# Row maxima of two heads in one step, one head in each row half of the array

## The chip, the cores and the metric

The kernel runs on one core of a Trainium2 chip. The metric is the device time of one execution in microseconds (us). Three runs of the kernel before took 3167.71, 3168.49 and 3175.28 us; the median is 3168.49 us.

## The reference, cut to what matters

Four residual layers work on 2048 rows of 512 numbers. Layers one and three (A) are attention with 32 query heads and one shared key/value head. Layers two and four (B) have 32 heads of 16 numbers each and cut the rows into 4 segments of 512: within a segment the attention is causal, and a running memory of the earlier segments is mixed in. The change touches only B's causal part:

```
for s in range(N):                                    # N = 4 segments of L = 512 rows
    qs, ks, vs = q[:, :, s], k[:, :, s], v[:, :, s]
    logits = jnp.einsum("bhqd,bhkd->bhqk", qs, ks) * scale + mask
    p = _softmax(logits, axis=-1)
    a_dot = jnp.einsum("bhqk,bhkd->bhqd", p, vs)
    ...
    o = g * a_mem + (1.0 - g) * a_dot
```

The logits of B are large, so the kernel needs the maximum of each row of logits (each head, each of the 512 rows of a segment, over the keys up to that row) before it takes exponentials.

## The kernel before, in words

**The work.** Rows come in 4 blocks of 512 (a block is a segment of B). One block of layer B, with the output projection of A ahead of it and its own behind it, is a "side" (`side`, L1182). Seven of the eight sides are woven with the scores and products of layer A for the next block (`weave`, L427); the eighth runs alone at the end. In a side B's 32 heads form 8 units of 4 heads, n = 0 to 7. The four heads j of a unit are (u, i), j = 2u + i: i says in which row half of the array the head's numbers lie (partitions 0 to 47 or 64 to 111 of `qkb`), u which of two column buffers it uses.

**The row maxima** (`b_rowmax`, L964; `b_rowmax_masked`, L942, in the last side). Query rows go in four tiles qt of 128, and tile qt meets nk = 128(qt+1) keys. For a head and a tile, `by_pairs` (L110) with one half issues four matmuls of 32 columns each, which write one PSUM bank: 48 rows of one row half of the array, four column groups. VectorE then reduces the bank. Unmasked, this is an instruction pair per head and tile (L988: add the causal mask, take the maximum into `mo`, then read the accumulator into `m`), 16 pairs for a unit. A job is what shares one bank: `(3, j)` with 512 keys; `(2, j)` and `(0, j)` with 384 and 128; two heads of tile 1 with 256 each. That makes 10 jobs for a unit, each with a bank of its own. In the last side the mask is added by four more matmuls (`maskw`), and VectorE needs a plain reduction (L959), 12 for a unit.

**The guard.** `guard_rows` (L681) transposes the maxima on TensorE (L687), VectorE splits them into two fp16 numbers (L690 to L693), and DMAs over `mf` put them into rows 48 and 49 of the half of `qkb` that each head uses. Only then can `b_attend` (L999) issue the scores of that unit (50 rows, `by_pairs` with both halves, eight matmuls into two banks, mask by `maskv`), the exponentials on ScalarE (L1027, `pa`), the products with the values (`b_pv`, L1068, reading `vb`) and the transposes on VectorE (L1038, L1047).

**The banks.** A ring hands out PSUM: "sc" holds two-bank slots for scores, "r" single banks for everything else (projections, row maxima, guards, products, transposes). `layout` (L359) gives "r" two banks (4 and 5) while a side is woven with A, eight at the start of the last side and four in the rest of it.

**What sets the order.** The program is written once, by a planner that keeps a clock per engine. Each generator yields the time at which its next step could start (`Need`, L371; a bank is ready HOP = 250 after the planned end of its reduction); `par` (L386), `step` and `weave` choose the next step by these times, by the array's tiling form and by how far A and the side have come. The row maxima of unit n+2 are planned beside unit n (`b_block`, L1138). Planned costs: `cols(nk)` per head and tile on TensorE, 65 + 1.05 per key on VectorE. Engines run their instructions in the order in which this leaves them, apart from a reach of 400 that `together` (L96) gives to the later matmuls of a group.

Of the kernel before, what the change touches and what calls it, by code (L numbers as in the profile page):

```python
# [31 lines left out]
BF16 = mybir.dt.bfloat16  # L32
# [3 lines left out]
ALU = mybir.AluOpType  # L36
AX = mybir.AxisListType

P = 128
# [50 lines left out]
def net_kernel(ctx, tc, x_in, a_wq, a_wk, a_wv, a_wo, b_wq, b_wk, b_wv, b_wo, b_beta, cst, out):  # L90
    nc = tc.nc
    V, A, G = nc.vector, nc.scalar, nc.gpsimd
# [3 lines left out]
    def together(first, *a, **k):  # L96

        if first:
            nc.tensor.matmul(*a, **k)  # L99
        else:  # L100
            with tc.high_priority(offset=400):
                tc.keep_in_program_order(nc.tensor.matmul(*a, **k))  # L102

    def by_columns(first, out_, lhsT, rhs, **k):

        for c in (2, 3, 0, 1):
            r_ = slice(32 * c, 32 * c + 32)
            together(first and c == 2, out_[r_], lhsT=lhsT[:, r_], rhs=rhs, **k)

    def by_pairs(out_, lhsT, rhs, rows=49, halves=(0, 1), mask=None):  # L110

        o = lambda r_, i: out_[r_, i] if len(halves) == 2 else out_[r_]
        for c in (2, 3, 0, 1):
            r_ = slice(32 * c, 32 * c + 32)
            for i in halves:
                w_ = slice(64 * i, 64 * i + rows)
                together(c == 2 and i == halves[0], o(r_, i), lhsT=lhsT[w_, r_], rhs=rhs[w_], start=True, stop=mask is None)
        if mask is None:
            return
        m_, a = mask  # L120
        for c in (2, 3, 0, 1):
            r_ = slice(32 * c, 32 * c + 32)
            for i in halves:
                w_ = slice(64 * i, 64 * i + 64)
                together(False, o(r_, i)[:, a:a + P], lhsT=idb[w_, 64 * i:64 * i + 32], rhs=m_[w_, c, :],
                         start=False, stop=True)

    def by_triangle(first, out_, lhsT, rhs):
# [19 lines left out]
    def nm(s):  # L148
        uid[0] += 1
        return f"{s}_{uid[0]}"  # L150

    def st(shape, dt, tag):
        return one.tile(shape, dt, tag=tag, name=nm(tag))

    def tmp(n, shape, dt, tag):
        return pools[n].tile(shape, dt, tag=tag, name=nm(tag))
# [5 lines left out]
    HOP = 250.0  # L162
# [10 lines left out]
    def pe(cost, form="full"):  # L173
        clk["pe"] += cost + (DRAIN if form != tiling[0] else 0.0)
        tiling[0] = form
        return clk["pe"]

    def on(engine, after, cost):
        clk[engine] = max(clk[engine], after + HOP) + cost
        return clk[engine] - NEAR[engine]  # L180
# [24 lines left out]
    maskq = st([P, 512], BF16, "maskq")  # L205
# [3 lines left out]
    idb = st([P, P], BF16, "idb")  # L209
# [8 lines left out]
    maskw = st([P, 4, P], BF16, "maskw")  # L218
# [116 lines left out]
    def cols(n, passes=1):  # L335
        return max(n * passes / 2.4, 107.0) + 3

    class Ring:
# [2 lines left out]
        def __init__(self, slots):  # L341
            self.slots, self.free = slots, [0.0] * len(slots)

        def ready(self):
            return min(self.free) + HOP

        def take(self):
            i = min(range(len(self.free)), key=lambda j: self.free[j])
# [8 lines left out]
    rings = {}  # L357
# [323 lines left out]
    def guard_rows(m, q, ring, exact):  # L681

        k, ps = ring.take()
        if len(ps.shape) == 3:
            ps = ps[:, 0, :]
        ps = ps[0:16, 0:P]
        T.transpose(ps, m.rearrange("p a b -> p (a b)"), ident)  # L687
        if not exact:
            mr = tmp(2, [16, 2, P], F16, "mrr")
            V.tensor_scalar_mul(mr[:, 0, :], ps, 1.0 / GUARD_K)  # L690
            V.scalar_tensor_tensor(mr[:, 1, :], ps, 1.0 / GUARD_K, mr[:, 0, :], op0=ALU.mult, op1=ALU.subtract)
            V.tensor_reduce(mmx[:, 1:2], ps, axis=AX.X, op=ALU.max, apply_absolute_value=True)
            V.tensor_tensor(mmx[:, 0:1], mmx[:, 0:1], mmx[:, 1:2], op=ALU.max)  # L693
            md = dram.tile([2, 16, P], F16, tag="mf" + str(uid[0] % 4), name=nm("mf"))
            nc.sync.dma_start(md.rearrange("o t c -> t o c"), mr)
            for i in range(2):
                nc.sync.dma_start(q[64 * i + 48:64 * i + 50].rearrange("o u (t c) -> o u t c", t=4),
                                  md.rearrange("o (u i t) c -> i o u t c", u=2, i=2)[i])
            t = on("dve", pe(110, "full"), 700)
            ring.free[k] = t  # L700
            return t + 2 * LOAD
        mr = tmp(2, [16, 2, P], BF16, "mrr")
        V.tensor_copy(mr[:, 0, :], ps)
        V.tensor_tensor(mr[:, 1, :], ps, mr[:, 0, :], op=ALU.subtract)
        md = dram.tile([2, 16, P], BF16, tag="md" + str(uid[0] % 4), name=nm("md"))
        nc.sync.dma_start(md.rearrange("o t c -> t o c"), mr)
        nc.sync.dma_start(q[96:98].rearrange("o j c -> o (j c)"), md.rearrange("o t c -> o (t c)"))
        t = on("dve", pe(110, "cols"), 350)
        ring.free[k] = t
        return t + 2 * LOAD  # L710
# [231 lines left out]
    def b_rowmax_masked(n, need):  # L942

        q, k = qb[n % 3], kb[n % 3]
        m = tmp(2, [P, 2, 2, 4], F32, "m")
        for qt in (3, 2, 1, 0):
            nk = (qt + 1) * P
            per = min(512 // nk, 2)
            for i in range(2):
                for u0 in range(0, 2, per):  # L950
                    yield Need(lambda: max(need, rings["r"].ready()), "rows")
                    ring = rings["r"]
                    s, ps = ring.take()
                    for u in range(per):
                        o_ = u * nk
                        by_pairs(ps[:, o_:o_ + nk], q[:, u0 + u, qt * P:(qt + 1) * P], k[:, u0 + u, 0:nk], 48, (i,),
                                 (maskw, nk - P))
                        e = pe(cols(nk) + 57, "rows")
                    V.reduce_max(m[:, u0:u0 + per, i, qt], ps[:, 0:per * nk].rearrange("p (h k) -> p h k", k=nk), axis=AX.X)  # L959
                    ring.free[s] = on("dve", e, 65 + 1.05 * per * nk)  # L960
        yield rings["r"].ready
        gr[n] = guard_rows(m.rearrange("p u i t -> p (u i) t"), q, rings["r"], False)

    def b_rowmax(n, need, exact=False):  # L964

        q, k = (qx, kx) if exact else (qb[n % 3], kb[n % 3])
        m = tmp(2, [P, 4, 4], F32, "m")
        jobs = [[(3, j)] for j in range(4)] + [[(2, j), (0, j)] for j in range(4)] + [[(1, 0), (1, 2)], [(1, 1), (1, 3)]]
        for job in jobs:
            yield Need(lambda: max(need, rings["r"].ready()), "cols" if exact else "rows")  # L970
            ring = rings["r"]
            s, ps = ring.take()
            o_ = 0
            for qt, j in job:
                nk = (qt + 1) * P
                if exact:
                    by_columns(o_ == 0, ps[:, o_:o_ + nk], q[0:96, j, qt * P:(qt + 1) * P], k[0:96, j, 0:nk],
                               start=True, stop=True)
                else:
                    u, i = divmod(j, 2)  # L980
                    by_pairs(ps[:, o_:o_ + nk], q[:, u, qt * P:(qt + 1) * P], k[:, u, 0:nk], 48, (i,))
                o_ += nk
                e = pe(cols(nk), "cols" if exact else "rows")
            o_ = 0
            for qt, j in job:
                nk = (qt + 1) * P
                mo = tmp(1, [P, 512], BF16, "mo")
                V.tensor_tensor_reduce(out=mo[:, 0:nk], in0=ps[:, o_:o_ + nk], in1=maskq[:, 512 - nk:512],  # L988
                                       op0=ALU.add, op1=ALU.max, scale=1.0, scalar=-3.0e38,
                                       accum_out=m[:, j, qt:qt + 1])  # L990
                o_ += nk
                e = on("dve", e, 65 + 1.05 * nk)
            ring.free[s] = e
        yield rings["r"].ready
        gr[n] = guard_rows(m, q, rings["r"], exact)

# [99 lines left out]
    def b_block(b, last, exact, norms):  # L1096
# [8 lines left out]
        def rowmax(*units):  # L1105
            for n in units:
                if n < 8:
                    need = b_load(hold[n // 2], n)
                    yield from b_rowmax(n, need, True) if exact else (b_rowmax_masked if last else b_rowmax)(n, need)
# [131 lines left out]
    ps = one_[0][0:1, 0:1]  # L1241
# [35 lines left out]
```

## Time and profile before

| | |
|---|---|
| median of three runs | 3168.49 us |
| the profiled execution | 3173.05 us, of which its span is 3170.8 us |
| granted TensorE clock, mean | 0.974 |
| busy: PE, ScalarE (ACT), VectorE (DVE) | 2804.4, 2328.1, 1553.0 us |
| row maxima on DVE: L988 (56 units of the seven woven sides) | 896 reductions, 438.7 us |
| row maxima on DVE: L959 (8 units of the last side) | 96 reductions |

PE is TensorE's matmuls, PEld its weight loads. The time that a wait took stands behind the group or instruction that waited, with what it waited for. Matmul durations in the trace are from the start to the modelled end of one matmul, and neighbouring ones overlap; how fast the array takes work is read from the distance between starts. The prediction shows the rows on which it rests.

### The profile page before, as it was taken

Reading aid. Unit: us, or ns where it says so; the run is one execution under the profiler, and the core shown is the slowest. Engines: PE = TensorE matmul, PEld = TensorE weight load, DVE = VectorE, ACT = ScalarE, POOL = GpSimd, SP = SyncE. Lnnn points to the kernel's source line nnn. Section 1 sums busy time; section 2 is a strip of 40 time slices with the busy share of each in tenths; the row PEclk is TensorE's granted clock in tenths of the full one; section 3 lists DMA queues with packets and bytes.
Section 4 is the critical chain, followed back from the end, with each engine's and each line's share of the span. In section 5 each row is a group of like instructions: output and inputs, shape, how many; then the busy total and the mean of one; then the engine's idle time right before and its main releaser. Section 6 shows DMA issues by size and latency. Waiting matters only on the chain.

```text
span 3170.8 us, 115988 instructions
## 1 busy us (share of the span) xinstructions
PE 2804.4 (88%) x51714; PEld 1329.7 (42%) x51714; DVE 1553.0 (49%) x4463; ACT 2328.1 (73%) x2583; POOL 269.5 (8%) x437
## 2 busy tenths in 40 slices
PE   7978898899888998889998898988998899888987
PEld 3533344344443454334443344443443434433543
DVE  7611345534565445554365545564345533654465
ACT  4699787886788867887788878767687876878423
POOL 3100120001000010001100010000000000000011
PEclk9999999999999999999999999999999999999978
DMA  5310231123311233102321142320331114110331
GB/s 157 113 61 20 75 111 45 38 64 100 91 48 29 67 108 93 48 16 93 122 85 50 35 143 86 111 67 23 112 94 36 38 49 127 46 48 22 121 99 34
DMA packets 147837, 231.84 MB, mean 73 GB/s; under 512 B 29728, under 2 KB 97152, under 8 KB 147328
## 3 DMA queue, kind: packets, MB, share of 16 engines
q1 hardware_dynamic: 118912, 121.56, 13.2%
q0 software_dynamic: 28416, 102.77, 10.1%
q8 instruction: 407, 6.67, 0.9%
q14 instruction: 102, 0.84, 0.1%
HBM read 162.12 MB, written 62.13 MB: 71 GB/s over the span
## 4 chain that ended last, share of the span: by engine, by line
PE 34%; ACT 27%; issue 22%; DVE 9%; DMA 5%; POOL 2%; SPq 1%; DVEq 0%; ACTq 0%; POOLq 0%
ACT pa L751 23%; PE bank L99 15%; PE bank L454 11%; PE bank L102 7%; DVE mo L988 4%; ACT pa L1027 3%; DMA sb<-parts 2%; DVE m L959 1%; DVE parts L552 1%; DMA xt<-in_A_x_dram 1%; DMA qkb<-sb 1%; POOL parts L550 0%; POOL w L275 0%; DMA w<-wd 0%; PE bank L687 0%
## 5 line engine op out<-in xcount | busy, mean ns | idle before, releaser
L751 ACT ACTIVATE pa<-bank 128x1024 f32<-128x1024 f32 x2048 | 1946.6, 1111 | 468.5 <-PE bank L102 464.4
L102 PE MATMUL bank<-pa,va 64*17 64x512 f32 x14336 | 1107.9, 602 | 0.2 <-DVE t L790 0.2
L99 PE MATMUL bank<-pa,va 64*17 64x512 f32 x2048 | 1065.0, 601 | 8.9 <-DVE ts L789 4.6
L99 PE MATMUL bank<-qa,kst 49*32 49x512 f16 x2048 | 745.0, 383 | 173.2 <-ACT pa L751 144.2
L102 PE MATMUL bank<-qa,kst 49*32 49x512 f16 x14336 | 825.1, 388 | 1.7 <-DVE qmx L599 1.7
L988 DVE CUSTOM_DVE_ANT_0 mo<-bank,maskq 128x256 bf16<-128x256 f32 (+3 forms) x896 | 438.7, 490 | 239.6 <-PE bank L102 177.8
L99 PE MATMUL bank<-qkb 48*32 48x512 f16 (+7 forms) x1536 | 347.7, 310 | 114.0 <-DVE m L988 44.9
L102 PEld LDWEIGHTS <-kst 49*32 49x32 f16 x14336 | 228.4, 90 | 496.3 <-issue 485.6
L1027 ACT ACTIVATE pa<-bank 128x1024 f32<-128x1024 f32 (+2 forms) x384 | 323.0, 887 | 139.5 <-PE bank L102 137.1
L102 PE MATMUL bank<-qkb 48*32 48x384 f16 (+7 forms) x6656 | 370.4, 313 | 0.0
L99 PEld LDWEIGHTS <-kst 49*32 49x32 f16 x2048 | 173.6, 92 | 370.9 <-issue 345.0
L454 PE MATMUL bank<-xh,w 128*128 128x512 f32 x832 | 284.4, 406 | 8.5 <-DVE w L318 5.0
L102 PEld LDWEIGHTS bank<-pa,va 64*17 64x17 f32 x14336 | 258.9, 95 | 25.5 <-DVE t L790 9.1
L454 PE MATMUL bank<-w,xh 128*128 128x512 f32 x752 | 247.8, 409 | 4.7 <-issue 3.1
L102 PEld LDWEIGHTS <-qkb 48*32 48x32 f16 (+1 forms) x6656 | 153.7, 94 | 202.7 <-issue 194.3
L99 PEld LDWEIGHTS bank<-pa,va 64*17 64x17 f32 x2048 | 186.6, 94 | 103.2 <-issue 18.2
L99 PEld LDWEIGHTS <-qkb 48*32 48x32 f16 (+1 forms) x1536 | 130.2, 95 | 172.5 <-issue 139.0
L789 DVE STREAM_TRANSPOSE ts<-bank 128x512 f32<-128x512 f32 x88 | 62.9, 714 | 276.4 <-PE bank L102 276.0
L275 POOL DMA_DIRECT2D w<-wd x154 | 85.4, 554 | 1253.2 <-PE bank L454 1166.7
L454 PEld LDWEIGHTS bank<-xh,w 128*128 128x128 f32 x832 | 156.8, 189 | 76.2 <-issue 29.7
L102 PE MATMUL bank<-pa,vb 128*17 128x384 f32 (+3 forms) x1920 | 173.9, 444 | 8.6 <-ACT pa L1027 7.7
L1038 DVE STREAM_TRANSPOSE t<-bank 128x512 f32<-128x512 f32 x64 | 45.9, 717 | 249.8 <-PE bank L102 249.8
(164 smaller groups left out, 2776.9 us busy)
## 6 DMA issues: line engine op xcount, KB each, us to landing
w<-wd POOLq DMA_DIRECT2D x154, 512.0 KB, 5.0
sb<-parts SPq DMA_DIRECT2D x128, 128.0 KB
qkb<-sb SPq DMA_DIRECT2D x256, 64.0 KB
wd<-w POOLq DMA_DIRECT2D x24, 512.0 KB, 4.1
x<-xt SPq DMA_DIRECT2D x48, 256.0 KB
xt<-x SPq DMA_DIRECT2D x48, 256.0 KB
qa<-sd SPq DMA_DIRECT2D x176, 66.0 KB
xt<-in_A_x_dram SPq DMA_DIRECT2D x32, 256.0 KB
```

The costliest lines, as they stand in the source:

```text
L99: nc.tensor.matmul(*a, **k)
L102: tc.keep_in_program_order(nc.tensor.matmul(*a, **k))
L275: G.dma_start(f(w), parts_d[kind, i])
L454: T.matmul(ps, lhsT=l_(kt), rhs=r_(kt), start=n == 0, stop=n == 11)
L552: V.scalar_tensor_tensor(parts[:, 1, :], x, up, parts[:, 0, :], op0=ALU.mult, op1=ALU.subtract)
L751: A.activation(x, sc, AF.Exp, scale=scale)
L789: V.transpose(ts.rearrange("p a b -> p (a b)"), pva[:, 0, :])
L959: V.reduce_max(m[:, u0:u0 + per, i, qt], ps[:, 0:per * nk].rearrange("p (h k) -> p h k", k=nk), axis=AX.X)
L988: V.tensor_tensor_reduce(out=mo[:, 0:nk], in0=ps[:, o_:o_ + nk], in1=maskq[:, 512 - nk:512], op0=ALU.add, op1=ALU.max, scale=1.0, scalar=- ...
L1027: A.activation(e[:, :, 0:w], sc[:, :, 0:w], AF.Exp, scale=0.25 if exact else 0.25 / (UPB * UPB))
L1038: V.transpose(t1.rearrange("p a b -> p (a b)"), pvb)
```

## The change

A new helper, `by_halves`, issues the matmuls of the two heads i = 0 and i = 1 of a column buffer alternately, head 0 into one single bank and head 1 into another. The row maxima take two single banks at a time, wait until two are free (`Ring.ready(n)` returns the time of the n-th free bank), issue the eight matmuls for each tile (and in the last side the eight mask matmuls), and reduce the first bank and then the second. A unit has 5 such steps in place of 10 jobs (6 in place of 12 in the last side). The number of matmuls and of reductions and their shapes stay the same. The branch `exact`, a fallback that isn't run on these inputs, keeps its jobs. The planner charges a step the TensorE time of one job and two reductions on VectorE.

```
+    def by_halves(outs, lhsT, rhs, rows, mask=None):
+
+        for c in (2, 3, 0, 1):
+            r_ = slice(32 * c, 32 * c + 32)
+            for i in range(2):
+                w_ = slice(64 * i, 64 * i + rows)
+                together(c == 2 and i == 0, outs[i][r_], lhsT=lhsT[w_, r_], rhs=rhs[w_], start=True, stop=mask is None)
...
-        def ready(self):
-            return min(self.free) + HOP
+        def ready(self, n=1):
+            return sorted(self.free)[n - 1] + HOP
...
-            for i in range(2):
-                for u0 in range(0, 2, per):
-                    yield Need(lambda: max(need, rings["r"].ready()), "rows")
-                    ring = rings["r"]
-                    s, ps = ring.take()
...
+            for u0 in range(0, 2, per):
+                yield Need(lambda: max(need, rings["r"].ready(2)), "rows")
+                ring = rings["r"]
+                got = [ring.take() for _ in range(2)]
+                for u in range(per):
+                    o_ = u * nk
+                    by_halves([g[1][:, o_:o_ + nk] for g in got], q[:, u0 + u, qt * P:(qt + 1) * P], k[:, u0 + u, 0:nk],
+                              48, (maskw, nk - P))
+                    e = pe(cols(nk) + 57, "rows")
+                for i, (s, ps) in enumerate(got):
...
+        two = not exact
+        if two:
+            jobs = [[(3, j)] for j in (0, 2)] + [[(2, j), (0, j)] for j in (0, 2)] + [[(1, 0), (1, 2)]]
...
-                    u, i = divmod(j, 2)
-                    by_pairs(ps[:, o_:o_ + nk], q[:, u, qt * P:(qt + 1) * P], k[:, u, 0:nk], 48, (i,))
+                    by_halves([g[1][:, o_:o_ + nk] for g in got], q[:, j // 2, qt * P:(qt + 1) * P], k[:, j // 2, 0:nk], 48)
...
+            for i, (s, ps) in enumerate(got):
+                o_ = 0
+                for qt, j in job:
```

The instructions move as follows. First TensorE in the first woven side, where unit 0's jobs of 384 and 128 keys stand (`qkb_27` holds that unit's queries and keys; the rows left out are the weight loads and the further matmuls of the same group). Before, four matmuls of 384, four of 128, and again four and four for the other head:

```order
L99 MATMUL bank<-qkb_27_131 32x384
...
L99 MATMUL bank<-qkb_27_131 32x128
...
L99 MATMUL bank<-qkb_27_131 32x384
...
L99 MATMUL bank<-qkb_27_131 32x128
...
L99 MATMUL bank<-qa_26_130,kst_21_121 32x512
```

Now eight of 384 and eight of 128:

```order
L99 MATMUL bank<-qkb_27_131 32x384
...
L102 MATMUL bank<-qkb_27_131 32x384
...
L99 MATMUL bank<-qkb_27_131 32x128
...
L102 MATMUL bank<-qkb_27_131 32x128
...
L99 MATMUL bank<-qa_26_130,kst_21_121 32x512
```

The two heads' groups, which stood one behind the other, are merged; the score group of layer A (`qa`, `kst`) follows both. Next VectorE in the last side, the row maxima of unit 4 (`m_53545`) with the transposes of unit 2's products (`t`), before:

```order
L959 TENSOR_REDUCE m_53545<-bank 128x1
L1065 STREAM_TRANSPOSE otb_155<-obb_53149 128x512
L959 TENSOR_REDUCE m_53545<-bank 128x1 x7
L959 TENSOR_REDUCE m_53545<-bank 128x2 x4
L1038 STREAM_TRANSPOSE t_5275_53852<-bank 128x512
L690 TENSOR_SCALAR mrr_53827<-bank 16x128
```

And now:

```order
L976 TENSOR_REDUCE m_53545<-bank 128x1
L710 TENSOR_TENSOR mmx_117<-mmx_117 16x1
L976 TENSOR_REDUCE m_53545<-bank 128x1 x3
L1059 STREAM_TRANSPOSE t_5273_53738<-bank 128x512
L1062 COPY rr_53740<-t_5273_53738 128x16
L1068 STREAM_TRANSPOSE t_5275_53746<-bank 128x512
L976 TENSOR_REDUCE m_53545<-bank 128x1
...
L976 TENSOR_REDUCE m_53545<-bank 128x2 x4
L707 TENSOR_SCALAR mrr_53862<-bank 16x128
```

Before, all twelve reductions of the unit stood ahead of the transposes; now four stand ahead of them and eight behind. On TensorE the products (`b_pv`) that the transposes wait for moved in the same way, from behind all row maxima of the unit to behind the first two steps.

More of the change, by code (lines that the diff above doesn't have):

```diff
@@ L125, in by_pairs @@
                 together(False, o(r_, i)[:, a:a + P], lhsT=idb[w_, 64 * i:64 * i + 32], rhs=m_[w_, c, :],
+                         start=False, stop=True)
+    def by_halves(outs, lhsT, rhs, rows, mask=None):
[4 more added lines that the diff above has]
+                together(c == 2 and i == 0, outs[i][r_], lhsT=lhsT[w_, r_], rhs=rhs[w_], start=True, stop=mask is None)
+        if mask is None:
+            return
+        m_, a = mask
+        for c in (2, 3, 0, 1):
+            r_ = slice(32 * c, 32 * c + 32)
+            for i in range(2):
+                w_ = slice(64 * i, 64 * i + 64)
+                together(False, outs[i][r_, a:a + P], lhsT=idb[w_, 64 * i:64 * i + 32], rhs=m_[w_, c, :],
                          start=False, stop=True)
@@ L948, in b_rowmax_masked @@
             per = min(512 // nk, 2)
-            for i in range(2):
-                for u0 in range(0, 2, per):
-                    yield Need(lambda: max(need, rings["r"].ready()), "rows")
-                    ring = rings["r"]
-                    s, ps = ring.take()
[L954 to L958, printed above, removed]
+            for u0 in range(0, 2, per):
[8 more added lines that the diff above has]
+                for i, (s, ps) in enumerate(got):
                     V.reduce_max(m[:, u0:u0 + per, i, qt], ps[:, 0:per * nk].rearrange("p (h k) -> p h k", k=nk), axis=AX.X)
@@ L967, in b_rowmax @@
         m = tmp(2, [P, 4, 4], F32, "m")
-        jobs = [[(3, j)] for j in range(4)] + [[(2, j), (0, j)] for j in range(4)] + [[(1, 0), (1, 2)], [(1, 1), (1, 3)]]
+        two = not exact
+        if two:
+            jobs = [[(3, j)] for j in (0, 2)] + [[(2, j), (0, j)] for j in (0, 2)] + [[(1, 0), (1, 2)]]
+        else:
+            jobs = [[(3, j)] for j in range(4)] + [[(2, j), (0, j)] for j in range(4)] + [[(1, 0), (1, 2)], [(1, 1), (1, 3)]]
         for job in jobs:
-            yield Need(lambda: max(need, rings["r"].ready()), "cols" if exact else "rows")
+            yield Need(lambda: max(need, rings["r"].ready(1 + two)), "rows" if two else "cols")
             ring = rings["r"]
-            s, ps = ring.take()
+            got = [ring.take() for _ in range(1 + two)]
             o_ = 0
@@ L976, in b_rowmax @@
                 if exact:
-                    by_columns(o_ == 0, ps[:, o_:o_ + nk], q[0:96, j, qt * P:(qt + 1) * P], k[0:96, j, 0:nk],
+                    by_columns(o_ == 0, got[0][1][:, o_:o_ + nk], q[0:96, j, qt * P:(qt + 1) * P], k[0:96, j, 0:nk],
                                start=True, stop=True)
                 else:
-                    u, i = divmod(j, 2)
-                    by_pairs(ps[:, o_:o_ + nk], q[:, u, qt * P:(qt + 1) * P], k[:, u, 0:nk], 48, (i,))
+                    by_halves([g[1][:, o_:o_ + nk] for g in got], q[:, j // 2, qt * P:(qt + 1) * P], k[:, j // 2, 0:nk], 48)
                 o_ += nk
[L983 to L993, printed above, removed]
+                e = pe(cols(nk), "rows" if two else "cols")
+            for i, (s, ps) in enumerate(got):
+                o_ = 0
+                for qt, j in job:
+                    nk = (qt + 1) * P
+                    mo = tmp(1, [P, 512], BF16, "mo")
+                    V.tensor_tensor_reduce(out=mo[:, 0:nk], in0=ps[:, o_:o_ + nk], in1=maskq[:, 512 - nk:512],
+                                           op0=ALU.add, op1=ALU.max, scale=1.0, scalar=-3.0e38,
+                                           accum_out=m[:, j + i, qt:qt + 1])
+                    o_ += nk
+                    t = on("dve", e, 65 + 1.05 * nk)
+                ring.free[s] = t
         yield rings["r"].ready
```

## The prediction

> **What bounds the kernel now.** I read the page first, for the shares of the engines and the chain of waits; then the groups by shape, for what the row maxima cost; then the waits; then the timeline of one unit's row maxima in a woven side and of one unit in the last side.
>
> ```profile
> span 3170.8 us, 115988 instructions
> PE 2804.4 (88%) x51714; PEld 1329.7 (42%) x51714; DVE 1553.0 (49%) x4463; ACT 2328.1 (73%) x2583; POOL 269.5 (8%) x437
> PE 34%; ACT 27%; issue 22%; DVE 9%; DMA 5%; POOL 2%; SPq 1%; DVEq 0%; ACTq 0%; POOLq 0%
> ```
>
> No engine is full. PE is busiest, but the chain passes between PE and ACT: PE works in order, and whatever waits in its program holds back what stands behind. The row maxima on PE, by the first matmul of each group of four:
>
> ```profile
> L99 PE MATMUL bank<-qkb 48*32 48x512 f16 x256 | 84.5, 395 | 48.7 <-DMA qkb<-sb 25.5 <-DVE m L988 21.2 <-DVE rr L1051 0.9
> L99 PE MATMUL bank<-qkb 48*32 48x384 f16 x256 | 80.8, 345 | 18.8 <-DVE m L988 13.2 <-DVE m L959 4.4
> L99 PE MATMUL bank<-qkb 48*32 48x128 f16 x256 | 53.9, 227 | 0.1
> L99 PE MATMUL bank<-qkb 48*32 48x256 f16 x256 | 51.3, 282 | 11.5 <-DVE m L988 10.5
> ```
>
> So 256 groups of each width: 4 for each of 64 units, of which 8 units are the last side's. The durations overlap; the pace is read from the starts. This is a stretch of unit 0's maxima in the first woven side (PE, then ACT at that time):
>
> ```profile
> 458.25 0.32 PE L99 MATMUL bank<-qkb 48*32 48x384 f16 x1 [0.35 <-DVE m L988]
> 458.29 0.38 PE L99 MATMUL bank<-qa,kst 49*32 49x512 f16 x1
> 458.42 0.21 PE L99 MATMUL bank<-qkb 48*32 48x128 f16 x1
> 458.47 0.40 PE L102 MATMUL bank<-qa,kst 49*32 49x512 f16 x4
> ...
> 459.91 0.27 PE L99 MATMUL bank<-qkb 48*32 48x256 f16 x1
> 460.02 0.27 PE L99 MATMUL bank<-qkb 48*32 48x256 f16 x1
> 460.34 0.27 PE L99 MATMUL bank<-qkb 48*32 48x256 f16 x1
> 460.38 0.38 PE L99 MATMUL bank<-qa,kst 49*32 49x512 f16 x1
> 456.85 4.03 ACT L751 ACTIVATE pa<-bank 128x1024 f32<-128x1024 f32 x4 [0.58 <-PE bank L102]
> 461.02 1.94 ACT L751 ACTIVATE pa<-bank 128x1024 f32<-128x1024 f32 x2 [0.15 <-PE bank L102]
> ```
>
> Two things are to be seen. First, the halves already run beside each other: the 384 group takes one half at 458.25, and layer A's score group, which stands behind it and behind the 128 group, starts in the other half at 458.29, before the 128 group at 458.42. What the first half does later, A's remaining four matmuls, starts at 458.47. Only the 256 groups at 459.91 and 460.02 leave the other half empty. Second, ACT works through this stretch with a gap of 0.15 us: it has scores in hand, and PE's time is mostly hidden.
>
> **The woven sides, TensorE.** The change removes nothing from the work: the same matmuls in the same half. It removes the time in which one half works alone. A group of 384 takes 0.17 us (458.25 to 458.42), one of 256 takes 0.11 (459.91 to 460.02); in proportion 512 takes 0.22 and 128 takes 0.055. One group of each is 0.555 us, times 4, times 56 units, 124 us of half-array time. In the stretch above the shown groups take 0.17 + 0.055 + 3 x 0.11 = 0.56 us; with the fourth 256 group 0.67. The other half is empty for 0.04 + 0.22 + 0.04 = 0.30 of it. Taking that 45% for all, 56 us are worked alone, and running them in pairs saves half: 28 us of PE. That is the bound if all of it lies on the path; none of it does where ACT has work, as above. I take a sixth, nearer the row of ACT's gap than the whole: **-5 us** (0 to -28).
>
> On the overlap the Trainium skill says otherwise: TensorE: Matmul & The Clock Gate, Part 3 (Packing small matmuls), holds that matmuls start and end strictly in program order. The rows at 458.29 and 458.42 disagree: the later group started first. By that rule a half left empty would be lost whole each time; it is the third rival.
>
> **The woven sides, VectorE and the banks.** The reductions stay:
>
> ```profile
> L988 DVE CUSTOM_DVE_ANT_0 mo<-bank,maskq 128x512 bf16<-128x512 f32 x224 | 154.2, 688 | 151.9 <-PE bank L102 137.3 <-DVE m L988 0.2
> L988 DVE CUSTOM_DVE_ANT_0 mo<-bank,maskq 128x384 bf16<-128x384 f32 x224 | 124.6, 556 | 59.6 <-PE bank L102 37.5
> L988 DVE CUSTOM_DVE_ANT_0 mo<-bank,maskq 128x256 bf16<-128x256 f32 (+3 forms) x896 | 438.7, 490 | 239.6 <-PE bank L102 177.8
> L988 DVE DVE_READ_ACCUMULATOR2_ANT m<- 128x1 f32 x896 | 74.3, 83 | 0.0
> PE bank L99 <- DVE m L988: 44.9, 102, 1.5
> PE bank L687 <- DVE m L988: 13.6, 24, 1.3
> PE bank L99 <- ACT pa L751: 159.2, 443, 4.3
> ```
>
> There are two banks in this stage. Before, VectorE reduces one while PE fills the other. Now both are filled, then reduced, and PE may fill again only when the second reduction is over. For a 512 pair that is two reductions of 0.69 + 0.08, 1.5 us, then about 0.4 us for the fill (a 512 matmul lasts 0.395) and some 0.1 us for two handovers: a gap of 0.5 us on VectorE in each pair that was covered before. Behind PE's wait stand layer A's scores, which feed ACT, and A's products; with two score slots filled, ACT can go on for about two exponentials.
>
> Before, PE waited 102 + 24 = 126 times over 560 jobs, 58 us in all, 0.46 us each: 22% of the jobs. Now there are 280 steps. With the same share, 63 waits, each longer by 0.5 us: 63 x 0.96 = 60 us against 58, so **0**. The ends: the waits become fewer and stay as short, 63 x 0.46 = 29 us, a gain of 29; or all 126 stay and half of the refill is hidden, 126 x 0.25, a loss of 31.
>
> The planner's charges also shift the places of nearly everything behind the first maxima. That has no row; it is part of why the range is wide on both sides.
>
> **The last side.** Here "r" has four banks, and nothing of layer A covers a wait. The iteration of unit 2, from guard to guard:
>
> ```profile
> 3071.81 0.38 PE L687 MATMUL bank<-cs,m 128*16 128x128 f32 x1
> 3075.58 0.27 PE L99 MATMUL bank<-qkb 50*32 50x256 f16 x1 [0.29 <-ACT pa L1027]
> 3076.53 0.37 PE L99 MATMUL bank<-qkb 48*32 48x512 f16 x1
> 3082.65 1.04 PE L99 MATMUL bank<-pa,vb 128*17 128x512 f32 x1
> 3086.56 0.28 PE L687 MATMUL bank<-cs,m 128*16 128x128 f32 x1
> 3071.95 0.72 DVE L1038 STREAM_TRANSPOSE t<-bank 128x512 f32<-128x512 f32 x1 [4.23 <-PE bank L102]
> 3074.98 0.68 DVE L959 TENSOR_REDUCE m<-bank 128x1 f32<-128x512 f32 x1
> 3077.05 0.71 DVE L1065 STREAM_TRANSPOSE otb<-obb 128x512 f32<-128x512 f32 x1 [1.39 <-POOL obb L1063]
> 3077.69 5.57 DVE L959 TENSOR_REDUCE m<-bank 128x1 f32<-128x512 f32 x11
> 3086.70 0.72 DVE L1038 STREAM_TRANSPOSE t<-bank 128x512 f32<-128x512 f32 x1 [3.45 <-PE bank L102]
> ```
>
> The iteration lasts 14.75 us. PE cannot start the products (3082.65) before it has issued the last of the twelve maxima, which go at VectorE's pace; then VectorE stands still for 3.45 us until the products end. In the changed order four reductions stand ahead of the transposes and eight behind, and the products come after the first two steps. So the cycle becomes: the short score groups with the two steps between them, from 0.95 us (3075.58 to 3076.53) to 2; the products, 3.9 (3082.65 to 3086.56); VectorE's work on them, 3.0 (3071.95 to 3074.98); eight reductions at 5.57/11 = 0.51, 4.1; the transpose into `otb`, 0.7 in every second unit; the guard, 0.4 on PE. With 1.5 for the first and 0.35 for the transpose that makes 13.25: 1.5 us less. Four of the six units that overlap have no projection between them, 6 us; in the two that have one, the projection covered VectorE's work on the products before, and now stands behind the guard, so I count +0.5 each. **-5 us** (-12 to +5: from a cycle two microseconds shorter in all six units to no gain and that loss in full).
>
> **The sum.** -5 + 0 - 5 = -10 us on the profiled execution's 3173.05 us (span 3170.8 and 2.25 around it), 3163. That execution is 4.56 us above the median of 3168.49; the same -10 on the median gives **3158.5 us**. About 0.3%, 9.5 us, is what a measurement of this kernel can tell from no change, so the forecast lies just beyond it.
>
> **The rivals.**
>
> *It is hidden.* In the woven sides ACT's work sets the time and the pairs only shorten what nobody waits for; for it speaks ACT's gap of 0.15 us above, and that PE's first matmuls wait for it in 443 places, 159 us in all; against it, that PE has 34% of the chain and ACT 27%. The last side then gives -3 or less: 3163 to 3171, say 3166. The Trainium skill's TensorEngine Tiling (Array Packing), section PSUM Bottleneck, speaks for this rival and against the change: tiling speeds up TensorE and not the emptying of PSUM. The trace agrees here, 438.7 us of reductions that do not change.
>
> *It is slower: two banks at once where there are two.* A projection, a transpose or a product accumulator that holds one of banks 4 and 5 now keeps the whole step away, and each refill is bare. It decides if PE's waits for `m` pass the 58 us that they take now by more than the 10 us gained. At 126 waits longer by 0.25 us it is +31 - 10 = +21: 3190; at 0.17 us, +21 - 10, it is 3180. Against it: PE has A's groups between the steps.
>
> *A half left alone costs its whole time.* Then the 124 us shrink to 62, and with the last side 3168.5 - 62 - 5 = 3101 at most; with half of it covered by ACT, 3132. The rows at 458.29 and 458.42 speak against it.
>
> That the pairs do not run together can hardly be: the eight score matmuls of `qa` in the two halves start within 0.2 us above even with one half taken.
>
> **How the numbers follow.** Forecast 0.54, its own range 3145 to 3167; hidden 0.22; slower 0.19; whole loss of the half 0.05. Of the forecast's chance 0.38 lies beyond 3159 and 0.16 short of it. Faster: 0.38 + 0.05 = 0.43. Same: 0.16 + 0.22 = 0.38. Slower: 0.19. The range goes from 3138, which leaves out the last rival, to 3182, which takes in the milder half of the slower one and leaves out the other; together some 0.15 to 0.2 outside.
>
> **What would show it.** Right: in the last side the distance from guard to guard (now L704) falls from 14.75 to 13 to 13.5 us, and VectorE's wait ahead of the transposes is filled; in the woven sides PE's waits for the reductions (now L1009) are about half as many and twice as long, near 58 us in sum; the 256 groups no longer run alone. Wrong: waits for `m` well above 70 us (the slower rival), a last side as long as before, or woven sides that shrink by 20 us and more.

## The result, and the profile after

The changed kernel takes 3196.18 us in the median of six runs (3193.44 to 3200.18), the kernel before 3173.20 in six (3167.71 to 3179.41): 1.0071 times as long, 95% interval 1.0055 to 1.0086. The forecast was 3158.5 us and the range ended at 3182. The kernel after is slower, by 23 us, close to the +21 of the slower rival. The granted clock does not explain it: 0.975 after, 0.974 before.

The profiled execution takes 3195.44 us. The page of the kernel after:

```profile
span 3193.3 us, 115947 instructions
PE 2784.9 (87%) x51714; PEld 1310.5 (41%) x51714; DVE 1549.5 (49%) x4463; ACT 2333.8 (73%) x2583; POOL 269.4 (8%) x437
PE 39%; ACT 26%; issue 18%; DVE 13%; DMA 2%; POOL 2%; SPq 0%; DVEq 0%; ACTq 0%; POOLq 0%
```

The work is the same: as many matmuls, as many VectorE instructions, busy times within 1.5%. What moved is the chain: VectorE's share rises from 9% to 13%, PE's from 34% to 39%. PE is busy for 19.5 us less than before (2804.4), as pairs that run beside each other would make it, but it is idle for 42.0 us more (408.4 of its span, before 366.4). PE's waits for VectorE's reductions, in the view of waits (total us, times, longest us):

```profile
PE bank L99 <- ACT pa L768: 164.1, 455, 4.3
PE bank L102 <- DVE m L1009: 53.1, 100, 0.9
PE bank L704 <- DVE m L1009: 35.7, 43, 2.5
...
PE bank L99 <- DVE m L1009: 26.2, 40, 3.1
```

Before, there were 44.9 us in 102 waits at L99 and 13.6 in 24 at the guard. Now a third kind stands first among the reductions' rows, which before did not exist: L102, the *second* matmul of a step. Over all its rows PE waits 117.8 us in 188 places for an unmasked reduction, before 58.5 in 126. (One kind of wait went the other way: PE's first matmuls waited 25.5 us for the DMA into `qkb` before, and 6.9 after.) ScalarE pays for the added waits. It waited 464.4 us (321 times) for the scores of A before, and 137.1 (98) for those of B; in the kernel after:

```profile
ACT pa L768 <- PE bank L102: 476.1, 355, 10.8
ACT pa L1048 <- PE bank L102: 156.2, 108, 22.0
```

That is 31 us more. How it comes about can be seen in the timeline of a woven side, PE and VectorE first, then ScalarE (start us, duration us, in brackets the idle time before and its releaser):

```profile
587.80 0.37 PE L99 MATMUL bank<-qkb 48*32 48x512 f16 x1
...
587.89 0.69 DVE L1009 CUSTOM_DVE_ANT_0 mo<-bank,maskq 128x512 bf16<-128x512 f32 x1
588.51 0.08 DVE L1009 DVE_READ_ACCUMULATOR2_ANT m<- 128x1 f32 x1
588.65 0.41 PE L102 MATMUL bank<-qkb 48*32 48x512 f16 x7 [0.47 <-DVE m L1009]
...
588.67 0.39 PE L99 MATMUL bank<-qa,kst 49*32 49x512 f16 x1
...
589.11 0.69 DVE L1009 CUSTOM_DVE_ANT_0 mo<-bank,maskq 128x512 bf16<-128x512 f32 x1 [0.51 <-PE bank L102]
...
589.72 0.08 DVE L1009 DVE_READ_ACCUMULATOR2_ANT m<- 128x1 f32 x1
589.86 0.32 PE L99 MATMUL bank<-qkb 48*32 48x384 f16 x1 [0.37 <-DVE m L1009]
...
589.95 0.69 DVE L1009 CUSTOM_DVE_ANT_0 mo<-bank,maskq 128x512 bf16<-128x512 f32 x1
590.57 0.08 DVE L1009 DVE_READ_ACCUMULATOR2_ANT m<- 128x1 f32 x1
590.71 0.52 PE L102 MATMUL bank<-qkb 48*32 48x384 f16 x7 [0.53 <-DVE m L1009]
...
590.73 0.61 PE L99 MATMUL bank<-qa,kst 49*32 49x512 f16 x1
589.33 1.94 ACT L768 ACTIVATE pa<-bank 128x1024 f32<-128x1024 f32 x2 [0.53 <-PE bank L102]
591.71 1.94 ACT L768 ACTIVATE pa<-bank 128x1024 f32<-128x1024 f32 x2 [0.44 <-PE bank L102]
```

The step of 512 keys begins at 587.80 in the first bank, which has just come free. Its second matmul needs the other bank, whose reduction runs until 588.59; it starts at 588.65, and A's scores, which stand behind it, at 588.67. So the two heads, meant to run beside each other, start 0.85 us apart. ScalarE has then run dry for 0.53 us. The next step, 384 keys, waits for its first bank (589.86) and again for its second (590.71). One step waits twice, and as the plan issues a step whole, A's group does not come between the two waits.

Where the time lies: A's last exponential starts at 3008.9 us, before at 2971.6, 37.3 us later. From there to the end it is 184.4 us, before 199.2: 14.8 less. This mark stands ahead of the end of the woven sides. At the first guard of the last side (3063.96, before 3033.56) the loss is 30.4 us, and from that guard to the end the trace has 7.9 us less. In the last side, the iteration of unit 2:

```profile
3103.12 0.38 PE L704 MATMUL bank<-cs,m 128*16 128x128 f32 x1 [1.29 <-DVE m L976]
...
3105.70 1.04 PE L99 MATMUL bank<-pa,vb 128*17 128x512 f32 x1
...
3116.32 0.27 PE L704 MATMUL bank<-cs,m 128*16 128x128 f32 x1
```

From guard to guard it is 13.20 us, before 14.75. The products start 2.6 us behind the guard, not 10.8. VectorE's wait of 3.45 us ahead of the transposes (now L1059) has shrunk to 2.70 and is not filled; reductions now stand behind the products as well:

```profile
3104.92 0.67 DVE L976 TENSOR_REDUCE m<-bank 128x1 f32<-128x512 f32 x1
3105.83 1.29 DVE L976 TENSOR_REDUCE m<-bank 128x1 f32<-128x512 f32 x2 [0.24 <-PE bank L102]
...
3109.82 0.72 DVE L1059 STREAM_TRANSPOSE t<-bank 128x512 f32<-128x512 f32 x1 [2.70 <-PE bank L102]
...
3113.24 2.42 DVE L976 TENSOR_REDUCE m<-bank 128x1 f32<-128x384 f32 x5
```

### The profile page after: what moved, and what is told of

Same layout as the page of the kernel before. It is cut to its first block, busy times and chain, and to the rows that moved or that the text cites. A ratio compares the mean times of both kernels' runs of the same rounds, so it can differ in the third digit from the quotient of the medians.

```text
span 3193.3 us, 115947 instructions
## 1 busy us (share of the span) xinstructions
PE 2784.9 (87%) x51714; PEld 1310.5 (41%) x51714; DVE 1549.5 (49%) x4463; ACT 2333.8 (73%) x2583; POOL 269.4 (8%) x437
## 4 chain that ended last, share of the span: by engine, by line
PE 39%; ACT 26%; issue 18%; DVE 13%; DMA 2%; POOL 2%; SPq 0%; DVEq 0%; ACTq 0%; POOLq 0%
ACT pa L768 22%; PE bank L99 15%; PE bank L471 14%; PE bank L102 9%; DVE mo L1009 6%; ACT pa L1048 3%; DVE m L976 1%; DVE parts L569 1%; POOL parts L567 0%; DMA xt<-in_A_x_dram 0%; PE bank L704 0%; DMA sd<-parts 0%; PE bank L531 0%; DMA wst<-in_B_wq_dram 0%; DVE t L1059 0%
## 5 line engine op out<-in xcount | busy, mean ns | idle before, releaser
L102 PE MATMUL bank<-pa,va 64*17 64x512 f32 x14336 | 1098.4, 602 | 0.2 <-DVE t L807 0.2
L99 PE MATMUL bank<-pa,va 64*17 64x512 f32 x2048 | 1066.4, 601 | 7.4 <-DVE ts L806 3.9
L99 PE MATMUL bank<-qa,kst 49*32 49x512 f16 x2048 | 743.2, 383 | 174.5 <-ACT pa L768 149.1
L102 PE MATMUL bank<-qa,kst 49*32 49x512 f16 x14336 | 793.8, 387 | 0.7 <-DVE qmx L616 0.4
L102 PEld LDWEIGHTS <-kst 49*32 49x32 f16 x14336 | 216.9, 90 | 502.9 <-issue 491.8
L99 PE MATMUL bank<-qkb 50*32 50x128 f16 (+7 forms) x1024 | 282.7, 312 | 74.4 <-ACT pa L1048 26.4
L102 PE MATMUL bank<-qkb 50*32 50x512 f16 (+7 forms) x7168 | 291.0, 316 | 61.9 <-DVE m L1009 53.1
L99 PEld LDWEIGHTS <-kst 49*32 49x32 f16 x2048 | 172.6, 92 | 368.9 <-issue 344.1
L102 PEld LDWEIGHTS bank<-pa,va 64*17 64x17 f32 x14336 | 256.0, 95 | 27.5 <-DVE t L807 12.4
L102 PEld LDWEIGHTS <-qkb 50*32 50x32 f16 (+1 forms) x7168 | 131.1, 94 | 258.7 <-issue 248.6
L99 PEld LDWEIGHTS bank<-pa,va 64*17 64x17 f32 x2048 | 187.2, 94 | 99.9 <-issue 19.0
L102 PE MATMUL bank<-pa,vb 128*17 128x384 f32 (+3 forms) x1920 | 167.2, 439 | 4.3 <-ACT pa L1048 3.4
L471 PE MATMUL bank<-xl,w 128*128 128x512 f32 x416 | 164.4, 395 | 0.2 <-DVE xl L539 0.2
L471 PEld LDWEIGHTS bank<-w,xh 128*128 128x128 f32 x752 | 135.2, 188 | 61.0 <-issue 24.6
```

The source lines that it names most:

```text
L471: T.matmul(ps, lhsT=l_(kt), rhs=r_(kt), start=n == 0, stop=n == 11)
```

## The experiments

Theory one: the reductions are too slow for a ring of two banks when a step needs both. The plan takes a bank to be free too early, and PE, in order, waits twice in a step with A's scores behind it. Theory two: the step is charged the TensorE time of one job for two heads, and the planner mixes the sides worse. Ratios are to the kernel before, run beside it, with their 95% intervals. "Waits" are PE's for unmasked reductions, in sum; "A's end" is the start of A's last exponential; both come from the profiled execution.

### Each part alone

`last_only` is the kernel after with the woven sides' jobs as before:

```
-            jobs = [[(3, j)] for j in (0, 2)] + ...
-            yield Need(lambda: max(need, rings["r"].ready(1 + two)), ...)
+        jobs = [[(3, j)] for j in range(4)] + ...
+            yield Need(lambda: max(need, rings["r"].ready()), ...)
```

> The pairs only in the last side; the seven woven sides as before. Theory one (a step that takes both banks of a two-bank ring makes PE wait for two bare reductions): faster than before by 8 to 15 us, the last side's part of the trace of after. Theory two (the halved TensorE charge makes the planner mix the woven sides worse, waits or not): the same here, since the woven sides keep their order. A gain under 4 us speaks against both readings of the last side.

`sides_only` has the pairs in the woven sides, and `b_rowmax_masked` as before:

```
-            for u0 in range(0, 2, per):
-                yield Need(lambda: max(need, rings["r"].ready(2)), "rows")
+            for i in range(2):
+                for u0 in range(0, 2, per):
+                    yield Need(lambda: max(need, rings["r"].ready()), "rows")
```

> The pairs only in the seven woven sides; the last side as before. Both theories: slower than before by 30 to 37 us, the loss that stands in the trace up to layer A's last exponential. If it and the kernel with the pairs in the last side alone don't add up to the whole change within 8 us, the two parts act on each other.

`last_only`: 3166.40 us against 3174.17, 0.9977 (0.9964 to 0.9990); waits 57.0 us, A's end 2972.2. `sides_only`: 3201.11, 1.0095 (1.0070 to 1.0121); waits 120.4 us, A's end 3009.0. So the last side gains 7.8 us and the woven sides lose 27; together +19, the whole change +23. Both lie a little under what was expected (8 to 15, and 30 to 37). `sides_only` has the full delay at A's end, 37 us, and loses only 27 to 28: some 10 us of that delay are made up behind A's last exponential, without the pairs in the last side.

### Short reductions

Each unmasked reduction reads 16 columns in place of its 128 to 512, in the kernel before and after; the exponentials are scaled down so that they stay finite. Charges, and with them the plan, are those of the full kernels.

```
-  V.tensor_tensor_reduce(out=mo[:, 0:nk], in0=ps[:, o_:o_ + nk], in1=maskq[:, 512 - nk:512],
+  V.tensor_tensor_reduce(out=mo[:, 0:16], in0=ps[:, o_:o_ + 16], in1=maskq[:, 512 - nk:528 - nk],
...
-  A.activation(e[:, :, 0:w], sc[:, :, 0:w], AF.Exp, scale=... 0.25 / (UPB * UPB))
+  A.activation(e[:, :, 0:w], sc[:, :, 0:w], AF.Exp, scale=... 1e-6 * 0.25 / (UPB * UPB))
```

> The changed kernel, in which each unmasked reduction reads 16 columns in place of 128 to 512 (so the maxima of the woven sides are not over all keys, and the exponentials are scaled by a millionth to stay finite). The planner's charges and so the order stay. Theory one: PE's waits for these reductions shrink from 117 us to under 40, the woven sides lose their 36 us, and this kernel is faster than its counterpart made from the kernel before by 5 us or more (the last side's gain) or at least no slower. Theory two: still slower than that counterpart by 12 us or more.

> The kernel before with the same shortened reductions and scaled exponentials (maxima not over all keys). Theory one: PE's waits for the reductions go from 58 us to under 20, the time falls by 10 to 40 us. Theory two: little change, under 10 us. It is there to be compared with the shortened form of the changed kernel.

`short_after`: 3076.42 us, 0.9713 (0.9685 to 0.9740), A's end 2885.5. `short_before`: 3114.73, 0.9824 (0.9797 to 0.9851), A's end 2912.6. The waits of `short_after`:

```profile
PE bank L99 <- DVE m L1009: 10.7, 19, 2.6
...
PE bank L704 <- DVE m L1009: 3.7, 5, 1.5
...
PE bank L102 <- DVE m L1009: 2.6, 10, 0.3
```

With short reductions the waits are gone, 17.3 us in sum (7.9 in `short_before`), and the changed kernel is the faster one, by 38 us, of which 27 stand at A's end. The sign of the change hangs on the reductions. Their length costs 123.4 us at A's end after (3008.9 less 2885.5) and 59.0 before (2971.6 less 2912.6), a difference of 64. PE's waits for them fall by 100.5 us after and 50.6 before, a difference of 50. Theory one expected the order of the two kernels to turn; theory two would have left the order's loss in place. `short_before` gained 59 us, more than the 10 to 40 expected. Shorter reductions relieve VectorE for everything else too; the test shows that their length decides, and the rows of waits show where.

### Charges on TensorE

`charge2_after` is the kernel after with the step charged two jobs, `charge_half_before` the kernel before with a job charged half:

```
-                e = pe(cols(nk), "rows" if two else "cols")
+                e = pe(2 * cols(nk), "rows" if two else "cols")
```

```
-            e = pe(cols(nk), "cols" if exact else "rows")
+            e = pe(cols(nk) / 2, "cols" if exact else "rows")
```

> The changed kernel, where the planner charges a step in the woven sides the TensorE time of two jobs, as it did before. Theory one (bare reductions in a two-bank ring): within 10 us of the changed kernel, about 3190. Theory two (the halved charge): the woven sides come back to the kernel before, 3165 or less.

> The kernel before, where the planner charges a job in the woven sides half the TensorE time. Theory one: within 8 us of the kernel before. Theory two: slower than before by 15 us or more.

`charge2_after`: 3195.31, 1.0060 (1.0037 to 1.0082); waits 104.8 us. Theory two falls as the cause: its charge mended, the loss stays. But `charge_half_before` takes 3208.50, 1.0101 (1.0078 to 1.0123), where theory one had expected next to nothing and theory two a loss of 15 us or more: a cheaper charge does harm the unpaired kernel. Its waits:

```profile
PE bank L99 <- DVE m L988: 56.3, 131, 2.1
...
PE bank L687 <- DVE m L988: 24.0, 39, 1.3
```

They come to 80.3 us in 170 places, 22 us more than before, with 32 us more time. A likely reading is that a cheaper charge lets the unpaired plan, too, put maxima where their banks are still held. It is not all of it: PE is also busy for 9.8 us longer than before (2814.2), and its waits for ScalarE's `pa` come to 215 us in place of 195.

### Charges on VectorE

The plan charges 65 + 1.05 per key, 603 for 512 keys and 199 for 128. In the trace of the kernel after, two reductions of 512 in the stretch shown start 0.84 us apart (589.11 to 589.95). The charge below makes it 745 for 512 keys (the expectation says 735) and 411 for 128. If the plan frees banks too early, a larger charge should cure the pairs. With the same edit in both kernels:

```
-                    t = on("dve", e, 65 + 1.05 * nk)
+                    t = on("dve", e, 300 + 0.87 * nk)
```

> The changed kernel, where the planner charges a reduction 300 + 0.87 per key, near the distance that the trace shows between reductions (735 for 512 keys, 411 for 128), in place of 65 + 1.05 per key (603 and 199). Theory one, in the form that PE waits because the plan has the banks free too early: PE's waits for the reductions fall from 117 us to about half and the time by 15 to 30 us. In the form that the bare refill itself costs it, whatever the plan: waits fall but the time moves by less than 10 us. Theory two says nothing on it.

> The kernel before with the same truer charge for a reduction. If the plan's early banks cost time before as well, its 58 us of waits fall by half and the time by 5 to 15 us; else it stays within 5 us.

`dvecharge_after`: 3125.59, 0.9835 (0.9814 to 0.9857), 71 us less than the change without it, where 15 to 30 were expected. Waits:

```profile
PE bank L704 <- DVE m L1009: 25.3, 46, 1.0
PE bank L102 <- DVE m L1009: 21.0, 50, 1.4
PE bank L99 <- DVE m L1009: 17.2, 28, 3.4
```

The second matmul's row has fallen from 53.1 to 21.0 us; the sum is 75.1. `dvecharge_before`: 3189.94, 1.0036 (1.0018 to 1.0055), with waits of 42.1 us, less than before; it lost where a gain of 5 to 15 us, or nothing, was expected. So the charge does not help by itself: in the unpaired kernel fewer waits bought nothing.

### Late banks, and how far an order can fall by chance

Here the reduction's charge stays and only the bank is planned free later, in the kernel after (first) and before; `nudge_after` and `nudge_before` change the charge by 5, to get another order of the same kind:

```
-                ring.free[s] = t
+                ring.free[s] = t + 500
```

```
-                ring.free[s] = e
+                ring.free[s] = e + 300
```

```
-  ... 65 + 1.05 * nk
+  ... 60 + 1.05 * nk
```

> The changed kernel, where the planner holds the two banks of a step back by 500 ns longer in the woven sides, and charges VectorE as before. Theory one (PE waits because the plan takes the banks as free too early): like the kernel with the truer charge for reductions, 3125 to 3160, waits for the reductions under 85 us. If that kernel's 70 us came from VectorE's planned clock in other places, or from a lucky order: 3180 and more.

> The kernel before, with each bank of the unmasked maxima held back by 300 ns longer in the plan. Theory one: waits for the reductions fall under 45 us, and the time lies between 15 us below and 15 us above the kernel before, since later maxima also delay the sides. A time below 3150 would say that the pairs are not needed for the gain of the truer charge.

> The changed kernel with 5 ns less charged for each unmasked reduction: too little to carry anything, so it measures what another order alone does. Theory one: within 10 us of the changed kernel. If orders differ by chance as much as the kernels compared here, it lies 20 us or more away, and the loss of the change could be chance.

> The kernel before with 5 ns less charged for each unmasked reduction, for the same purpose: within 10 us of the kernel before if chance is small, 20 us or more away if it isn't.

| | us | ratio (95%) | waits, us | A's end, us |
|---|---|---|---|---|
| `bankdelay_after` | 3164.80 | 0.9967 (0.9949 to 0.9984) | 74.5 | 2980.4 |
| `bankdelay_before` | 3170.79 | 0.9993 (0.9979 to 1.0007) | 48.4 | 2974.5 |
| `nudge_after` | 3201.06 | 1.0082 (1.0060 to 1.0104) | 127.3 | 3016.8 |
| `nudge_before` | 3183.42 | 1.0029 (1.0016 to 1.0043) | 65.2 | 2983.9 |

Another order of the same kind moves the time by 5 to 11 us, in the two that were tried; the change's loss of 23 and the gains of 31 and 71 lie beyond that. The late bank gives back the loss, though it ends 5 us above the 3125 to 3160 expected (`bankdelay_before` has waits of 48.4 us where under 45 were expected). With the same waits as `dvecharge_after` it is 39 us slower; the sum of waits is not the whole price. The traces show where the rest lies. PE is busy for 2771.2 us in `bankdelay_after` and 2748.9 in `dvecharge_after`, 22 less, and its waits for ScalarE's `pa` come to 221 and 205 us, 17 less. In `dvecharge_before` the same two outweigh what the shorter waits gave: PE is busy for 10.1 us longer than before, and waits for `pa` 14 us longer. Part of the busy time may go with the granted clock, 0.978 and 0.982 in the first two.

### The dose

Is it a lucky order, or does it go with the charge? A charge halfway, the same charge nudged by 5, and a larger one, all in the kernel after:

```
-  ... 65 + 1.05 * nk
+  ... 180 + 0.96 * nk     (dvecharge_mid_after)
+  ... 295 + 0.87 * nk     (dvecharge_nudge_after)
+  ... 390 + 1.13 * nk     (dvecharge13_after)
```

> The changed kernel with the charge for a reduction half way from 65 + 1.05 to 300 + 0.87 per key (180 + 0.96). If the truer charge itself works, the time lies between the two, 3145 to 3180, with waits for the reductions between 75 and 118 us. If the 3125.6 us at the truer charge were a lucky order, no such place between is to be expected.

> The changed kernel with the truer charge less 5 ns for a reduction (295 + 0.87 per key). If the gain belongs to the charge: 3115 to 3140. If it belongs to one lucky order: nearer to the kernel that holds the banks back, 3150 to 3175.

> The changed kernel with the charge for a reduction 1.3 times the truer one (390 + 1.13 per key). If PE's waits are what costs: they fall below 75 us; the time is within 20 us of 3125, with what the later maxima cost the sides taken back from it. A time of 3165 or more with fewer waits would say that waits are not the whole of it.

| charge for 512 keys | kernel | us | ratio (95%) | waits, us | A's end, us |
|---|---|---|---|---|---|
| 603 | after | 3196.18 | 1.0071 (1.0055 to 1.0086) | 117.8 | 3008.9 |
| 672 | `dvecharge_mid_after` | 3152.03 | 0.9941 (0.9921 to 0.9962) | 88.3 | 2965.3 |
| 740 | `dvecharge_nudge_after` | 3128.04 | 0.9855 (0.9835 to 0.9876) | 70.6 | 2946.3 |
| 745 | `dvecharge_after` | 3125.59 | 0.9835 (0.9814 to 0.9857) | 75.1 | 2940.0 |
| 969 | `dvecharge13_after` | 3118.38 | 0.9824 (0.9805 to 0.9844) | 48.8 | 2933.1 |

The time falls with the charge, the waits nearly so (75.1 us at 745, 70.6 at 740), and the nudged plan agrees with its neighbour, so one lucky order does not explain it. `dvecharge13_after` has the lowest time of the full kernels here, 55 us below the kernel before and 78 below the change as it stood; its ratio's interval overlaps that of `dvecharge_after`. Its charge, 969, is above the 840 ns that the trace shows; what can be read from it is that a charge above the true one does no harm here. The kernel before was not run with it. Its page and waits:

```profile
span 3118.6 us, 115974 instructions
...
PE 37%; ACT 33%; issue 17%; DVE 8%; DMA 3%; POOL 1%; SPq 1%; ACTq 0%; POOLq 0%; DVEq 0%
```

```profile
PE bank L704 <- DVE m L1009: 14.2, 33, 0.6
...
PE bank L99 <- DVE m L1009: 12.3, 15, 3.6
PE bank L102 <- DVE m L1009: 10.3, 25, 1.0
```

```profile
ACT pa L768 <- PE bank L102: 435.3, 254, 11.2
ACT pa L1048 <- PE bank L102: 127.7, 86, 21.9
```

VectorE's share of the chain is 8% in place of 13%, and ScalarE waits 69 us less for scores than in the kernel after (563.0 in place of 632.3).

## Why the prediction was wrong, by its own steps

**The step that failed** is the second term, VectorE and the banks, set at 0. It said: 280 steps, the old share of 22%, so 63 waits of 0.96 us, 60 us in sum. The runs show 188 waits and 117.8 us. The count failed. The prediction held that PE "may fill again only when the second reduction is over" and took a step for a job, with one place to wait. A step has two, its first matmul for one bank and its second for the other, and the second alone waits 100 times, 53.1 us. The guard waits more as well, 35.7 us for 13.6. And the old share of 22% belonged to a plan that asked for every bank by itself. One by one the waits are shorter than the 0.96 us assumed, 0.63 (117.8 / 188), but there are three times as many as the 63, and half again as many as before. A reduction was counted as 0.69 + 0.08 us, too; from start to start it is 0.84. The term's upper end, +31 with 126 waits, kept the old count too.

**The first term**, TensorE at -5 (0 to -28), was mis-sized: with the reductions shortened A's end comes 27 us earlier, the far end of the range. The stretch in which I read a gap of 0.15 us on ScalarE was one where PE was ahead, and I let it stand for all. The bound was too low for that stretch as well: just ahead of the lines shown a group of 384 and one of 128 keys start, at 457.50 and 457.66, and the next start in the other half is that at 458.29; the 45% leaves them out. The 27 us are not TensorE's alone. Between the two short kernels PE is busy for 39.1 us less (2778.4 to 2739.3), waits for the DMA into `qkb` 13.7 us less and for ScalarE's `pa` 15 us more, and some of it may go with the granted clock (see below).

Put together, A's end is -27 by the pairs with short reductions and +64 by the reductions' length, +37 in the trace. These figures make 37 by their construction. What supports them is that the waits for the reductions, read by themselves, differ by 50 us of the 64 (and some 16 of it may be the clock's, see below), and that mending the plan alone turns the sign.

**The third term**, the last side, came out near: -5 predicted, -7.8 measured alone, 13.20 us from guard to guard in unit 2's iteration where 13.25 was worked out. That the sum fits is in part luck. VectorE's wait was to be filled, and 2.70 us of it are left. From the side's first guard on, the seven distances between guards change by +0.64, +1.83, -1.56, -1.55 (the one shown), -0.33, -3.23 and -2.37 us; the third and the fifth hold most of the projection's matmuls, for which +0.5 each was counted.

**The rivals.** The one that came true is the slower one, two banks at once where there are two, by its own mark (waits for `m` above 68 us). Its price of 31 us, from 126 waits at 0.25, was half of the 59 us that came. That its total, +21, lies so near the measured +23 is luck: the gain on TensorE set against it was too small as well. The Trainium skill's TensorEngine Tiling (Array Packing), section Gotcha 1: PSUM Pressure, says that row tiling raises the pressure on PSUM, and that different row tiles write to different banks. The runs agree, with 53.1 us at the second bank. The prediction drew on the Trainium skill's section PSUM Bottleneck, under the same title, only as a reason for no change. "It is hidden" fell with the short kernels, "a half alone costs its whole time" by the size of the gain: 27 us and not 62.

**What stays open.** Why one order leaves PE busy longer and waiting longer for ScalarE than another with the same waits for the reductions, as in `dvecharge_before`, `bankdelay_after` and `charge_half_before`; and how much of it is the clock. No run gave the woven sides a third bank, which would test the cause most directly.

## What to carry to other kernels

A step that takes both banks of a ring of two has two places to wait: here its first head filled one bank while the other was still being reduced, and everything behind stood at the second. Count waits by bank, not by step, and ask what stands behind the second. When a change makes a plan lean on a figure that the old plan could miss without harm, here the time of a reduction, compare the figure with the trace first. The change and the mended charge together gained 50 us (`dvecharge_after`), while each by itself lost. What one half of the array does alone is read by taking away what may hide it, not from one stretch in which it was hidden.

## What the runs showed of the hardware

The granted TensorE clock differs from kernel to kernel, in the profiled executions: 0.974 before, 0.975 after, 0.978 in `short_before`, 0.985 in `short_after`, 0.981 to 0.983 in the paired kernels with a larger charge, 0.971 in `dvecharge_before`. It also goes with the time inside one kernel: of ten runs of `bankdelay_after` the fastest took 3152.80 us at 0.983, the slowest 3174.07 at 0.974, 0.7% for 0.9%. If the clock sets the time at that rate, up to 22 of the 55 us of `dvecharge13_after` come by way of its clock (0.9% more, by the same ratio), and some 16 of the 27 us between the short kernels' sides (0.7% more, so 0.55% of 2900 us); no run here fixed the clock, so which is cause stays open. Between before and after there is no such difference, and two kernels that lost had a higher clock than the kernel before: 0.980 in `charge2_after`, 0.978 in `nudge_after`.

A reduction of 512 keys holds VectorE for longer than its row says: 0.69 us and 0.08 for the read of the accumulator, but 0.84 from one start to the next (589.11 to 589.95). The read ends at 589.80, and the next bank had been written by 589.06, so the 0.15 us between are not a wait for PE. The median distance from a reduction of 512 keys to the next reduction in line is 844 ns before (183 of them) and 845 after (187).
